# Normalised tokens prepared by chunks of features instead of by tiles of tokens, and one vector made piece by piece, in a two-part transformer block

## The chip, the cores and the metric

The kernel runs on one core of a Trainium2 chip. The metric is the device time of one execution in microseconds. A core has a matrix engine (TensorE, PE in the profile; its weight loads are listed apart as PEld), VectorE (DVE), ScalarE (ACT), GpSimd (POOL) and SyncE (SP), which here only issues DMA transfers. Each engine works through its own row of instructions in order and waits on semaphores for the others. PE writes to PSUM, eight banks of 128 x 512 float32; the other data lie in SBUF, 128 partitions wide.

## The reference, cut to what matters

2048 tokens of 512 features (float32), one batch. `c` gives six vectors of 512 that shift, scale and gate.

```python
mod = (silu(c) @ w_mod).reshape(1, 6, 1, -1)
sa, ca, ga, sb, cb, gb = (mod[:, i] for i in range(6))
h = layernorm(x) * (1 + ca) + sa
x = x + ga * A(h, wq, wk, wv, wo, beta)
h = layernorm(x) * (1 + cb) + sb
x = x + gb * (relu(h @ w1 + b1) ** 2 @ w2 + b2)
# A: 32 heads of 16; the tokens in 4 segments of 512. In a segment: softmax attention with a mask,
# mixed by a gate with a read of a memory (M, z) that the earlier segments' keys and values have filled
# through phi(t) = t + 1 if t > 0 else exp(t); then the segment adds its own. At the end @ wo
```

The change is in the third line: how `layernorm(x) * (1 + ca) + sa` gets into the form that the products with `wq`, `wk` and `wv` read, and how `sa` is made.

## The kernel before, in words

**Numbers in two halves.** A product of float32 matrices is made from operands split in a high part (rounded by a copy to the type float32r) and a low part (what is left). Three matmuls add up: high x high, high x low, low x high.

**Segments and units.** The 512 tokens of a segment lie in four tiles of 128. A segment has four units of eight heads, so there are 16 units `u = 4*s + cc`. For each unit `qk` projects queries and keys (banks `bqk`), `vproj` makes the values of a segment (`bv`), `a_quad` computes scores for the row maxima (`ba`), `b_quad` the scores again, transposed, their exponentials (`pt`) and the products with the values (`bpv`), and `mem` reads and updates the memory (`bmr`, `bpkt`, `bmu`). Two other streams run beside this: `make_w1` prepares combinations of blocks of `w1` in the buffer `X1L`, each cast to a high part by ACT (line 747) and stored to `w1d` in DRAM, and the projected output of a segment goes to DRAM. After the last segment come `wo`, the second normalisation and the feed-forward part (`bh`, `bpf`), from about 440 us to the end.

**The first normalisation** (`ln1`). For each tile of 128 tokens DVE takes the statistics (`ln_stats`), POOL the reciprocal root, and DVE normalises in place (`ln_apply`; tile `xt`). Then `ln_transposed`, tile by tile: PE turns the four 128 x 128 blocks of the tile into one bank `blnq`; the result has the features on the partitions, in KD = 4 chunks of 128. Scale and shift then differ by partition and chunk, so `ln_affine` needs one instruction for each chunk, 128 columns wide: in segment 0 two on ACT and two on DVE, in the other segments all four on ACT (`lnf`). `ln_split` copies the high part into `HT` (ACT) and subtracts for the low part (DVE in segment 0, POOL later). `HT` is `[P, 2, KD, L]`: high and low, four chunks, 512 tokens. There is one `HT`, so the copies of a segment wait for all projections of the segment before (`HUSE[s - 1]`), and the projections wait for all eight halves (`HTN[s]`). Only unit 0 is different: it is made in two halves of 256 tokens.

**Scale and shift** (`mod_cols`). `mod_parts` multiplies the columns of `c` with `w_mod` in four column groups at once (bank `bmod`, 4 matmuls of 512 columns), ACT copies the four partial rows out, and four matmuls against a selecting column add them up and turn them (bank `bmodc`, 1 column each). This is done for the multiplier (`ca`, 1) and for the added vector (`sa`, 0).

**Order.** `Plan` holds every piece of work as a node with its engine, its predecessors and the buffers that it takes and gives back. The order in which an engine's nodes are written out comes from `ORDER`, a table of node numbers for each of PE, ACT, DVE, POOL and SP. At run time each engine keeps to that order, whatever is ready. `N_WARM = 70` nodes on PE are warm-ups, matmuls of the unit matrix that nobody reads (`bwarm`, line 542); the table places them, too. A product on half of the array's rows (projections and scores) waits, where the second turn begins, for a one-element copy on ACT (`fence`).

Of the kernel before, what the change touches and what calls it, by code (L numbers as in the profile page):

```python
# [17 lines left out]
P = 128  # L18
D = 512
# [38 lines left out]
8-32 3 33-43 94 86 117 96 88 111 44-47 123 48-49 105 50-77 280 290 281-282 291 283-286 292 287 293-297 447-449 333-334  # L58
450 335-336 868 452-454 350 364 455 873 338-340 371 341 379 606-609 385 361 392 611-612 358 613 355 614 316-319 376
367 321 551 322 476 481 323-324 382 732 397 733 400 388 734 404 735 490 407 737 497 738 505 412 878 883 508 739 484  # L60
740 487 416-418 395 420 427 554 522 502 423 430 524 493 435 439 677 635 511 440-441 640 887 556 888 646 563 889 559
890 443 566 892-893 643 571 894 514 895 649 656 530 575 680 576-577 670 579 532 586 1056 589 664 1057 582 1058 652
1059 761 769 803 1061-1062 594 775 598 806 546 599-600 682 996 689 1063-1064 692 920 667 921-922 661 923 548 766 685
925 673 926 772 697 927 782 928 790 778 701-703 705 602 937 712 938 954 939 962 715 940 1131 708 942 968 943 720
944-945 793 1481 724 1191-1192 808 796 1193-1194 787 999 1196-1197 811 799 1198-1199 975 989 725 1002 726 815 959 818
965 823 827 1266 980 831 828-829 834 1326 838 846 1327 971 1328 1089 1329 986 841 1486 1471 1331 983 1332-1333 1134
1097 1334 992 1476 728 1110 850 1137 851 1005 1124 852 1100 1118 1269 1008 1012 854 1015 1094 1024 1103 1020 1028 1025
1115 1035 1272 1026 1031 1106 1121 1038 1224 1235 1043 1047 1232 1238 1140 1048-1049 1143 1490 1147 1127 1491 1155
1150 1492 1229 1493 1051 1245 1159 1253 1163 1160-1161 1404 1166 1495 1170 1496 1259 1173 1497 1241 1498 1178 1401
1359 1182-1184 1275 1256 1540-1541 1282 1250 1542-1543 1278 1186 1285 1545-1546 1290 1364 1547 1262 1548 1380 1373  # L70
1523-1524 1367 1525 1388 1407 1294-1296 1370 1298 1526 1305 1385 1528 1301 1529 1391 1313 1530 1376 1531 1394 1659
1557 1660-1661 1565 1662 1308 1599 1664 1571 1665 1397 1666-1667 1602 1562 1317-1319 1794 1410 1413 1795 1321 1796
1578 1797 1586 2079 1568 1799 1417 1800 1425 1801 1574 1420 1802 1589 1592 2084 1429 1605 1430-1431 1734 1692 2074
1697 1929 1433 1930 1440 1931 1583 1436 1932 1443 1448 1703 2089 1452 1608 1595 1934-1935 1611 1700 1936 1713 1937
1706 1737 1453 1718 1615 1740 1454 1724 1618 1869 1623 1627 1721 1631 1709 1628-1629 1634 1727 1638 1641 1456 1872
1646 1650 1827 1835 1743 1651 1875 1652 1841 1750 2093 1753 1730 2094 1832 1746 2095 1758 2096 1848 1838 1762 1654
1766 1763-1764 1862 1769 2098 1856 1773 2099 1776 2100 1844 2101 1859 1781 2004 1785-1787 2007 1962 2122 1853 1878
2123 1885 2124 1865 1970 2125 1983 1888 2127 1789 1976 2128 1893 2129-2130 2251 1967 2252 1881 2253-2254 1973 2198
1997 538 1897-1899 1991 1901 2256 1908 2257 1979 2258 2156 1994 2259 2139 1904 2140 1988 2141 2161 2142 1911 2167 2144
2000 2145 1916 2170 2146-2147 2177 2191 1920-1922 540 2013 2188 2375 2016 2376 2164 2020 2377 2023 2378 1924 2185 2028  # L80
2380-2381 2173 2382 2301 2306 2383 2322 2182 2032-2034 2036 2499 2043 2500 2046 2309 2501 2194 2502 2315 2280 2504
2039 2505 2312 2506 2051 2285 2055 2201 2507 2288 2204 2056-2057 2291 2208 2318 2211 2059 2216 2220 2224 2227 2221
2231 2294 2010 2222 2234 2446 2239 2641 2243 2404 2297 2244-2245 2418 2651 2644-2647 2409 2325 2328 2654-2655 2661
2415 2332 2335 2656-2657 2340 2412 2247 2425 2344-2346 2348 2355 2439 2664 2671 2665-2667 2351 2421 2674 2681
2675-2677 2363 2528 2542 2684-2685 2721 2686 2536 2430 2358 2724 2687 2725-2727 2691 2436 2533 2449 2367-2369 2433
2456 2464 2694-2695 2731 2696-2697 2442 2459 2452 2371 2734 2701 2735 2774 2736 2549 2563 2539 2737 2468-2470 2472
2545 2479 2704-2705 2560 2475 2482 2706-2707 2487 2573 2554 2766 2741 2770 2762 2491-2493 2557 2576 2580 2744-2746
2583 2566 2570 2495 2588 2747 2711 2592 2596 2603 2593 2599 2606 2611 2714-2717 2751 2594 2615-2617 2754 2619
# [131 lines left out]
2396 2524 2680 2523 2525 2517 2670 2700 2720 2520 2519 2740 2522 2730 2424 2526 2690 2445 2710 2838 2548 2569 2750  # L220
2796-2797 2839 2843 2828 2798 2818 2884 2808 2847 2856 2848 2852 2861 2865 2857 2866 2874 2901 2875 2879 2870 2883
2893 2888 2892 2897 3167-3173 3424-3426 3379 3427-3430 3681-3682 3388 3131 3683 3639 3125 3645 3122 3684 3636 3685
3642 3382 3385 3128 3686-3687 3893 3896 3902 3899
""",
}

# [1394 lines left out]
```

## Time and profile before

| | |
|---|---|
| median of 3 runs | 764.79 us (761.73 to 765.94) |
| profiled execution | 762.98 us |
| its span, first to last instruction | 761.3 us |
| mean granted clock of PE | 0.995 |
| busy: PE, DVE, ACT, POOL | 749.7, 582.7, 440.1, 322.3 us |

The granted clock is the share of full speed that the chip allows PE. A row of the profile's lists names the line of the kernel, the engine, the operation and `out<-in` by the names of the tiles, with a count, times in us unless marked ns, and, behind a bar or in brackets, the idle time of that engine just before and what ended it. The chain that ended last is followed back from the last instruction, at each step to what released it. Windows give busy time by stretches of the span. A float32 matmul is recorded as two passes, so that 70 warm-ups are 140 records. Times of PE's records overlap a little; distances from start to start are safer to add up.

### The profile page before, as it was taken

How to read it: one execution, taken by the hardware profiler on the slowest of the kernel's cores; microseconds unless marked ns; L12 is line 12 of the kernel's file. 1: busy time of each engine (PE TensorE's matmuls, PEld its weight loads, DVE VectorE, ACT ScalarE, POOL GpSimd, SP SyncE). 2: the span in 40 equal slices, each digit the busy share in tenths (PEclk: the TensorE clock that was granted, in tenths of full speed). 3: DMA queues.
4: the chain of work that ended last, by engine and by line, in shares of the span. 5: the costliest groups of instructions: out<-in, count | busy, mean ns of one | idle time of the engine just before them, and what ended most of it. 6: DMA issues, size and time to landing. Idle time of an engine off the chain costs nothing.

```text
span 761.3 us, 18032 instructions
## 1 busy us (share of the span) xinstructions
PE 749.7 (98%) x6649; PEld 598.1 (79%) x6649; DVE 582.7 (77%) x1591; ACT 440.1 (58%) x1001; POOL 322.3 (42%) x400
## 2 busy tenths in 40 slices
PE   9999999999999999999999999999999999999997
PEld 8977676666687667766676679998998899989986
DVE  4587789888899788989989887868855875577544
ACT  2669888899878998678856844636111321221110
POOL 4667777677778777474422542350002002000000
PEclk9999999998999999999999999999999999999999
DMA  9587873554654425355753156753555254448621
GB/s 309 171 239 213 247 206 99 154 148 134 167 161 128 113 80 153 105 141 167 235 170 126 44 194 241 269 200 135 194 194 193 103 208 189 158 161 275 242 92 55
DMA packets 61057, 129.65 MB, mean 170 GB/s; under 512 B 8613, under 2 KB 23977, under 8 KB 59178
## 3 DMA queue, kind: packets, MB, share of 16 engines
q1 hardware_dynamic: 60818, 128.37, 52.8%
q8 instruction: 53, 0.87, 0.5%
q14 instruction: 34, 0.28, 0.1%
q10 hardware_dynamic: 152, 0.13, 0.1%
HBM read 81.29 MB, written 20.19 MB: 133 GB/s over the span
## 4 chain that ended last, share of the span: by engine, by line
PE 86%; ACT 4%; DMA 3%; SPq 2%; POOL 2%; issue 2%; DVE 1%; ACTq 0%; POOLq 0%; DVEq 0%
PE bh L1501 18%; PE bpv L1131 8%; PE bqk L796 7%; PE bpf L1564 7%; PE bpf L1563 7%; PE bpf L1565 7%; PE bpb L1072 5%; PE ba L903 5%; PE bv L869 5%; PE bwop L1233 2%; PE bwarm L542 2%; DMA w1d<-X1L 2%; PE bwop L1235 2%; PE bwop L1234 2%; PE blnq L613 2%
## 5 line engine op out<-in xcount | busy, mean ns | idle before, releaser
L908 DVE CUSTOM_DVE_ANT_0 ba<-ba,msk 128x384 f32<-128x384 f32 (+2 forms) x384 | 192.8, 531 | 34.5 <-PE ba L903 21.3
L1089 ACT ACTIVATE pt<-bpb 128x512 f32<-128x512 f32 x320 | 172.4, 621 | 18.4 <-PE bpb L1072 15.8
L1076 POOL TENSOR_SCALAR_AFFINE_SELECT pt<-pt 128x512 f32<-128x512 f32 x128 | 80.3, 645 | 84.2 <-ACT pt L1089 69.7
L796 PE MATMUL bqk<-HT,WQK 64*128 64x512 f32 x720 | 103.4, 398 | 0.0
L1131 PE MATMUL bpv<-pt,VT 128*32 128x512 f32 (+3 forms) x1024 | 81.5, 441 | 1.4 <-ACT pt L1089 0.9
L1072 PE MATMUL bpb<-ST 64*128 64x256 f32 (+2 forms) x512 | 78.5, 351 | 1.7 <-DVE mx L908 1.2
L796 PEld LDWEIGHTS bqk<-HT,WQK 64*128 64x128 f32 x720 | 68.8, 185 | 10.7 <-DVE mx L908 1.2
L903 PE MATMUL ba<-ST 63*128 63x256 f32 (+2 forms) x512 | 75.1, 346 | 1.5 <-ACT pt L1089 0.7
L1332 POOL TENSOR_TENSOR tt<-h2raw 128x512 f32<-128x512 f32 x8 | 10.9, 1367 | 142.6 <-ACT h2raw L1297 98.6
L1072 PEld LDWEIGHTS bpb<-ST 64*128 64x128 f32 x512 | 51.9, 189 | 21.4 <-ACT pt L1089 4.8
L903 PEld LDWEIGHTS ba<-ST 63*128 63x128 f32 x512 | 48.1, 187 | 24.0 <-ACT pt L1089 5.4
L1527 ACT COPY p<-bh 128x256 f32<-128x256 f32 x28 | 10.4, 371 | 93.1 <-PE bh L1501 64.9
L1501 PEld LDWEIGHTS bh<-ST,w 128*128 128x128 f32 x420 | 56.5, 189 | 3.5
L1501 PE MATMUL bh<-ST,w 128*128 128x256 f32 x420 | 59.0, 282 | 0.0
L1501 PE MATMUL bh<-ST 128*128 128x256 f32 x420 | 58.4, 282 | 0.0
L1501 PEld LDWEIGHTS bh<-ST 128*128 128x128 f32 x420 | 55.8, 190 | 3.1
L908 DVE DVE_READ_ACCUMULATOR2_ANT mx<- 128x1 f32 x384 | 54.2, 141 | 0.0
L1131 PEld LDWEIGHTS bpv<-pt,VT 128*32 128x32 f32 x1024 | 28.2, 109 | 32.8 <-issue 23.0
L1563 PE MATMUL bpf<-w,ST 128*128 128x512 f32 x136 | 53.8, 395 | 0.0
L1545 ACT CAST ST<-xx 128x512 fp32r<-128x512 f32 x43 | 26.1, 619 | 47.6 <-DVE xx L1537 19.1
L1564 PE MATMUL bpf<-w,ST 128*128 128x512 f32 x136 | 53.6, 394 | 0.0
L869 PE MATMUL bv<-WVO,HT 64*128 64x512 f32 x384 | 53.2, 396 | 0.0
(211 smaller groups left out, 1671.1 us busy)
## 6 DMA issues: line engine op xcount, KB each, us to landing
ST<-w1d SPq DMA_DIRECT2D x14, 1792.0 KB
w<-w1d SPq DMA_DIRECT2D x14, 1792.0 KB
ST<-sg SPq DMA_DIRECT2D x192, 128.0 KB
w1d<-X1L SPq DMA_DIRECT2D x21, 512.0 KB
xt<-in_A_x SPq DMA_DIRECT2D x16, 256.0 KB
wm<-in_w_mod SPq DMA_DIRECT2D x16, 256.0 KB
xw<-in_A_x SPq DMA_DIRECT2D x16, 256.0 KB
X1L<-in_B_w SPq DMA_DIRECT2D x7, 512.0 KB
```

The costliest lines, as they stand in the source:

```text
L796: nc.tensor.matmul(bank(banks[w]), W3(w, k, x, cols.start, cols.stop)[r], HT[r, y, k], start=turn == k == i == 0, stop=turn == 1 and k == ...
L869: nc.tensor.matmul(bank(banks[t]), HT[r, x, k, (t2 + t) * P:(t2 + t + 1) * P], WVO[r, k, y], start=turn == k == i == 0, stop=turn == 1 and ...
L903: nc.tensor.matmul(dst[:, c0:c0 + n], ST[b:b + 63, 0, sl, qt * P:(qt + 1) * P], ST[b:b + 63, 1, sl, :n], start=True, stop=True)
L908: nc.vector.tensor_tensor_reduce(i, i, msk[:, 512 - n:], scale=1.0, scalar=-3e38, op0=ALU.add, op1=ALU.max, accum_out=o)
L1072: nc.tensor.matmul(dst, ST[b:b + 64, 1, sl, kb * P:(kb + 1) * P], ST[b:b + 64, 0, sl, q0:512], start=True, stop=True)
L1076: nc.gpsimd.affine_select(out=ap, in_=ap, pattern=[[0, ap.shape[1]], [1, P]], compare_op=ALU.is_ge, fill=0.0, base=0, channel_multiplier=-1)
L1089: ns = [op("ACT", 0.49, lambda j=j: nc.scalar.activation(buf("PPP"[n], pt)[:, i + j], bank(keys[j]), AF.Exp, scale=0.25), pr[slot] + 0.01 ...
L1131: nc.tensor.matmul(bank(o)[32 * hq:32 * hq + 32, q0:q0 + src.shape[1]], v[:, a:a + 32], src, start=start, stop=stop, tile_position=(0, 32 ...
L1501: nc.tensor.matmul(pb(i), A[:, x, kk], B[:, y, kk], start=kk == j == 0, stop=kk == 1 and j == 2)
L1563: nc.tensor.matmul(q, rh, wh, start=(i == 0), stop=False)
L1564: nc.tensor.matmul(q, rh, wl, start=False, stop=False)
L1565: nc.tensor.matmul(q, rl, wh, start=False, stop=(i == NF - 1))
```

## The change

**By chunks.** `ln1` normalises all four tiles first. Then `ln_chunk`, for each chunk of 128 features: PE turns this chunk's block of all four tiles into one bank (still 16 transposes in a segment), one instruction scales and shifts all 512 tokens (ACT; in segment 0 DVE for chunks 1 and 3), ACT copies the high part and DVE or, from segment 1, POOL subtracts. A turn now waits for the normalisation of all four tiles.

**Readers.** A projection's products with chunk `k` wait for that chunk alone (`HTK[s][k]`), and a chunk's high half waits only for the last readers of the same chunk in the segment before (`HKUSE[s - 1][k]`). `chunk` sets in which order a segment reads the chunks, up or down, so that the chunk that is read last differs from segment to segment. Unit 0 reads 512 tokens at once: 24 matmuls of 512 columns in place of 48 of 256.

**Added vector.** `mod_pieces` makes `sa` without the detour: as each 128 rows of `w_mod` have landed, four matmuls with one column of `c` add to four columns of a bank, 16 in all, weights 128 x 128; there is no copy by ACT.

**Order.** All five tables are new, 3894 nodes in place of 3905. Three places show how.

At the start, PE, from the first product for `bmod` on, before. `blnq` is the bank of the turned blocks, `bqk` of the projections:

```order
L570 MATMUL bmod<-wmod,cs 32x512 x8
L613 MATMUL blnq<-ident,xt 128x128 x4
L592 MATMUL bmodc<-selc,t 128x1 x8
L613 MATMUL blnq<-ident,xt 128x128 x4
L542 MATMUL bwarm<-ident 128x128 x4
L613 MATMUL blnq<-ident,xt 128x128 x4
L542 MATMUL bwarm<-ident 128x128 x2
L613 MATMUL blnq<-ident,xt 128x128 x4
L542 MATMUL bwarm<-ident 128x128 x28
L788 MATMUL bqk<-HT,WQK 128x256
```

The same place now, from the last of the pieces on:

```order
L608 MATMUL bmodc<-cs,wmod 128x1 x4
L542 MATMUL bwarm<-ident 128x128 x3
L570 MATMUL bmod<-wmod,cs 32x512 x4
L542 MATMUL bwarm<-ident 128x128 x4
L592 MATMUL bmodc<-selc,t 128x1 x4
L640 MATMUL blnq<-ident,xt 128x128 x16
L542 MATMUL bwarm<-ident 128x128 x23
L804 MATMUL bqk<-HT,WQK 128x512 x3
L542 MATMUL bwarm<-ident 128x128 x11
L804 MATMUL bqk<-HT,WQK 128x512 x3
L542 MATMUL bwarm<-ident 128x128 x3
L804 MATMUL bqk<-HT,WQK 128x512 x3
```

The sixteen turns now stand together, behind the multiplier's two steps. Of the 70 warm-ups 28 stand ahead of `bmod` (36 before), 27 between it and the first projections (34 before), and 15 among the products of the first chunks (none before).

ACT in the normalisation of segment 2, before. `X1L` is the cast for the feed-forward weights, `pk`, `mt`, `ac`, `sg` are copies for the memory, the maxima, the scores and the projections:

```order
L747 CAST X1L<-X1L 128x256
L1089 ACTIVATE pt<-bpb 128x512 x2
L619 ACTIVATE lnf<-blnq,modc 128x128 x8
L1024 COPY pk<-bpkt 128x4x64 x2
L747 CAST X1L<-X1L 128x512
L970 ACTIVATE mt<-bat 16x64 x2
L626 CAST HT<-lnf 128x4x128
L619 ACTIVATE lnf<-blnq,modc 128x128 x4
```

The same place now:

```order
L644 ACTIVATE lnf<-blnq,modc 128x512
L763 CAST X1L<-X1L 128x256
L1039 COPY pk<-bpkt 128x4x64
L650 CAST HT<-lnf 128x512
L1039 COPY pk<-bpkt 128x4x64
L985 ACTIVATE mt<-bat 16x64 x2
L650 CAST HT<-lnf 128x512
L951 COPY ac<-ba_2750 128x512
L951 COPY ac<-ba_2749 128x512
L650 CAST HT<-lnf 128x512
L841 CAST sg<-bqk 128x512 x2
L763 CAST X1L<-X1L 128x512
```

The 512-column cast of `X1L` has moved behind three copies to `HT`, two to `ac` and two to `sg`.

PE in the normalisation of segment 1, before, the third and fourth tile's turns:

```order
L1072 MATMUL bpb<-ST 128x256 x4
L613 MATMUL blnq<-ident,xt 128x128 x8
L903 MATMUL ba_1058<-ST 128x512
L903 MATMUL ba_1059<-ST 128x512
L796 MATMUL bqk<-HT,WQK 128x512 x6
```

Now three of the four chunks' turns stand in one piece, ahead of other score products:

```order
L1087 MATMUL bpb<-ST 128x256 x2
L1087 MATMUL bpb<-ST 128x384 x2
L640 MATMUL blnq<-ident,xt 128x128 x12
L918 MATMUL ba_965<-ST 128x256
L918 MATMUL ba_966<-ST 128x256
```

The first two tiles' turns stood far earlier before, apart from each other; now no turn stands before the fourth tile is normalised.

The diff, without the tables:

```diff
@@ ORDER @@
-8-32 3 33-43 94 86 117 96 88 111 44-47 123 48-49 105 50-77 280 290 281-282 291 283-286 292 287 293-297 447-449 333-334
+8-24 3 25-28 94 29 95-96 30-32 97 33-35 86 36-39 88 117 121 109 113 40-62 283 63-73 284 74-76 285 77 277-280 286
...
+    def mod_pieces(m, slot, plus, pr):
+        key, b = ("wmod", m), ("modc", m)
+        loads, n = [], None
+        for k in range(KD):
+            loads.append(sp(lambda k=k: nc.sync.dma_start(buf("P", key)[:, k] if not k else TL[key][:, k],
+                                                          wmod[k * P:(k + 1) * P, m * D:(m + 1) * D]),
+                            pr + 0.001 * k, 1 << 18, get=() if k else [("P", key)], soft=loads[:1]))
+
+        def mm(k):
+            for j in range(KD):
+                nc.tensor.matmul(bank(b)[:, j:j + 1], TL[key][:, k, j * P:(j + 1) * P], cs[:, k:k + 1],
+                                 start=k == j == 0, stop=k == j == KD - 1)
+        for k in range(KD):
+            n = pe("F", 1.05, lambda k=k: mm(k), pr + 0.02 + 0.001 * k, after=[n_cs, loads[k], n], get=() if k else [("#D", b)],
+                   put=[key])
+        return dve(4, lambda: nc.vector.tensor_scalar(modc[:, slot, :], bank(b)[:, 0:KD], plus, None, op0=ALU.add),
+                   pr + 0.05, after=[n], put=[b])
...
+    def ln_chunk(s, k, pr, applied, wait):
+
+        b, f = ("lnq", s, k), ("lnf", s, k)
+        keys = [("xt", 4 * s + t) for t in range(4)]
+
+        def turn():
+            for t in range(4):
+                nc.tensor.transpose(bank(b)[:, t * P:(t + 1) * P], TL[keys[t]][:, k * P:(k + 1) * P], ident)
+        n = pe("F", 0.357, turn, pr, after=applied, get=[("#D" if s else "#A", b), ("oraw", f)], put=keys)
+        sc, bi = modc[:, CA, k:k + 1], modc[:, SA, k:k + 1]
+        if s or k % 2 == 0:
+            n = act(512, lambda: nc.scalar.activation(buf("oraw", f), bank(b), AF.Identity, scale=sc, bias=bi), pr + 0.01,
+                    after=[n, *MODC[CA]], put=[b])
...
+            n = dve(512, lambda: nc.vector.tensor_scalar(buf("oraw", f), bank(b), sc, bi, op0=ALU.mult, op1=ALU.add), pr + 0.01,
+                    after=[n, *MODC[CA]], put=[b])
+        eng, e = (nc.gpsimd, "POOL") if s else (nc.vector, "DVE")
+        h = act(512, lambda: nc.scalar.copy(HT[:, 0, k], TL[f]), pr + 0.02, sbuf=True, after=[n, *wait], put=[f])
+        l = op(e, 1.24 if s else 0.6, lambda: eng.tensor_tensor(HT[:, 1, k], TL[f], HT[:, 0, k].bitcast(F32), op=ALU.subtract), pr + 0.03,
+               after=[h], put=[f], lock=True)
         return [h, l]
...
-    n_sa = mod_cols(0, SA, 0.0, PR0 + 0.2, True)
+    n_sa = mod_pieces(0, SA, 0.0, PR0 + 0.2)
...
+    HTK, HKUSE = {}, {s: [[] for _ in range(KD)] for s in range(-1, NS)}
+
+    def chunk(s, turn, i):
+
+        return KD - 1 - i if (s + turn) % 2 else i
...
+        HTK[s] = {}
+        for i in range(KD):
+            k = chunk(s, 0, i)
+            HTK[s][k] = ln_chunk(s, k, p_turn[i], ap, HKUSE[s - 1][k])
...
-                    n = pe("R", 0.697, lambda turn=turn, k=k: half(turn, KD - 1 - k if turn else k), pr[turn] + 0.002 * k,
-                           after=[n] if n else [*HTN[s], *(z for w in (0, 1) for z in (WN[w, cc] if s == 0 else []))],
...
+                    n = pe("R", 0.697, lambda turn=turn, k=k, i=i: half(turn, k, turn == i == 0, turn == 1 and i == KD - 1), pr[turn] + 0.002 * i,
+                           after=[n, *(HTK[s][k] if not turn else ()),
...
-            for i in range(0 if u else 2):
-                c = slice(i * L // 2, (i + 1) * L // 2)
...
+            for k in range(0 if u else KD):
+                n = done[w] = pe("F", 0.697, lambda w=w, k=k: mm(w, k), pr[w] + 0.002 * k,
+                                 after=[done.get(w), *HTK[0][k], *(WN[w, cc] if k == 0 else []), *([] if k or w else [n_w0])],
```

`vproj` is changed in the same way as `qk`.

393 lines of the change are left out of this document (182 added, 211 removed), and 14 rows, old and new, of the table ORDER.

## The prediction

> **What bounds the kernel now.** I read the page first: span, busy time and the shares of the chain that ended last.
>
> ```profile
> span 761.3 us, 18032 instructions
> ...
> PE 749.7 (98%) x6649; PEld 598.1 (79%) x6649; DVE 582.7 (77%) x1591; ACT 440.1 (58%) x1001; POOL 322.3 (42%) x400
> ...
> PE 86%; ACT 4%; DMA 3%; SPq 2%; POOL 2%; issue 2%; DVE 1%; ACTq 0%; POOLq 0%; DVEq 0%
> ```
>
> PE is the bound almost everywhere: 98% busy, 86% of the chain. So the change can gain only where PE runs slowly or the chain leaves it, and it loses wherever it adds to PE. Next I cut the span into windows. The columns are window, length, busy time (and instructions) of PE, PEld, DVE, ACT and POOL, granted clock, DMA share, GB/s.
>
> ```profile
> 60.00:80.00 20.00, 19.64 (x241) 13.66 (x237) 17.26 (x59) 19.89 (x53) 14.33 (x16) 1.00 0.80 239
> ...
> 160.00:180.00 20.00, 18.84 (x232) 10.55 (x229) 16.32 (x63) 17.55 (x40) 13.73 (x20) 0.83 0.37 107
> ...
> 240.00:260.00 20.00, 20.00 (x218) 13.98 (x216) 15.62 (x48) 19.53 (x48) 15.44 (x18) 1.00 0.49 129
> 260.00:280.00 20.00, 19.62 (x284) 12.37 (x284) 17.06 (x65) 20.00 (x48) 16.26 (x23) 1.00 0.19 45
> 480.00:520.00 40.00, 40.00 (x261) 36.34 (x260) 29.06 (x59) 22.83 (x45) 17.40 (x15) 1.00 0.64 230
> ```
>
> ACT is full at 60 to 80 and at 240 to 280 us, and at 160 to 180 the granted clock is only 0.83. These are the three places where segments 1, 2 and 3 are normalised. In the feed-forward part (480 to 520) PE has no idle time and nothing to win. The chain in order of time (start, length, what) runs through the scaling of the normalised tokens, tile `lnf`, at all three:
>
> ```profile
> 69.03 1.90 ACT lnf L619 x6
> ...
> 70.93 0.89 ACT lnf L619 x2
> ...
> 163.03 0.82 ACT lnf L619 x3
> ...
> 163.97 0.44 ACT lnf L619
> ...
> 258.52 1.50 ACT lnf L619 x4
> ```
>
> That is 5.55 us of the chain in 16 instructions, four groups of four. The slow clock comes in two steps; finer windows show them:
>
> ```profile
> 160.20:163.60 3.40, 2.92 (x40) 1.74 (x36) 3.19 (x14) 2.56 (x9) 3.04 (x5) 1.00 0.84 212
> 163.60:167.00 3.40, 3.01 (x70) 1.44 (x62) 1.58 (x4) 3.07 (x8) 2.98 (x7) 1.00 0.67 217
> 167.00:169.90 2.90, 2.61 (x20) 1.45 (x16) 2.83 (x12) 2.90 (x7) 1.07 (x1) 0.99 0.03 6
> 169.90:173.30 3.40, 3.40 (x31) 2.50 (x30) 2.95 (x13) 3.38 (x9) 1.64 (x3) 0.50 0.00 0
> 173.30:176.70 3.40, 3.40 (x19) 1.42 (x18) 2.64 (x9) 2.26 (x6) 2.47 (x3) 0.50 0.00 0
> ```
>
> PE is idle for 0.48, 0.39 and 0.29 us in three windows running, and then for 6.8 us the clock is at half. PE's timeline names who was late, and ACT's what held it:
>
> ```profile
> 162.47 0.60 PE L903 MATMUL ba<-ST 63*128 63x256 f32 x4 [0.47 <-ACT mt L970]
> ...
> 164.46 0.46 PE L1033 MATMUL bmu<-VT,pk 128*32 128x34 f32 x32 [0.39 <-ACT lnf L619]
> ...
> 167.81 1.12 PE L903 MATMUL ba<-ST 63*128 63x512 f32 x5 [0.27 <-ACT pt L1089]
> ```
> ```profile
> 156.12 0.41 ACT L747 CAST X1L<-X1L 128x256 fp32r<-128x256 f32 x1
> ...
> 157.40 2.90 ACT L619 ACTIVATE lnf<-blnq,modc 128x128 f32<-128x128 f32 x8
> ...
> 161.68 0.62 ACT L747 CAST X1L<-X1L 128x512 fp32r<-128x512 f32 x1 [0.84 <-DMA w1d<-X1L]
> ```
>
> All three waits are for ACT, behind eight scalings in a row and a cast that waits 0.84 us for a store of feed-forward weights to land.
>
> **The change, part by part.** *Added vector by pieces.* Before, both vectors took two steps on PE:
>
> ```profile
> 12.43 1.92 PE L570 MATMUL bmod<-wmod,cs 128*32 128x512 f32 x16
> ...
> 14.78 1.84 PE L592 MATMUL bmodc<-selc,t 128*128 128x1 f32 x16
> ...
> 18.73 0.60 PE L613 MATMUL blnq<-ident,xt 128*128 128x128 f32 x4
> ...
> 19.17 6.42 PE L542 MATMUL bwarm<-ident 128*128 128x128 f32 x56
> ...
> 22.66 1.93 DVE L626 TENSOR_TENSOR HT<-lnf,HT 128x512 fp32r<-128x512 f32 x3 [0.30 <-ACT HT L626]
> ...
> 25.34 0.36 PE L788 MATMUL bqk<-HT,WQK 128*128 128x256 f32 x1
> ```
>
> Each row holds two vectors, so one vector cost 0.96 + 0.92 = 1.9 us. The pieces are 16 matmuls of the second row's own form (it shows 8, at two passes each): 16 x 1.84/8 = 3.7. PE does 1.8 us more. Does the start hide that? The warm-ups are fixed in number and order: 70 before, 70 after. So PE's stream up to the first projections is a sum, and what is added to it comes out behind it, unless PE waits less. It waited a little: the first row's 1.92 for 16 passes holds about 0.5 of waiting for late loads, while the pieces' loads now come first. I take +1.3 (bounds: +0.5, if all overlaps well; +1.8, if nothing is saved).
>
> *First projection over whole chunks.* 48 matmuls of 256 columns become 24 of 512. They ran from 25.34 to just after this row's last start:
>
> ```profile
> L790 PE MATMUL bqk<-HT,WQK x16: 279/283/283, 25.7 to 31.0; 128*128 128x256 f32 x16
> ```
>
> 5.7 us for 12,288 columns; the same columns again, so 0 (bounds -0.2, 0). Is `HT` ready in time? Before, 24.6 - 18.7 = 5.9 us passed from the last turn to the last low half (rows above). After, 23 warm-ups, at 6.42/28 = 0.23 each 5.3 us, lie before the first chunk's products, and 15 more among them; with three chunks' products (0.7 each) 10.8 us lie before the last chunk's. So readiness is covered, and the 15 warm-ups are time that PE spends although the operands are there. If that cover were gone, PE would wait, and warm-ups would only trade places with idle time.
>
> *Fourth tile's load.* It moves from sixth to tenth in SP's queue, behind four more loads of 0.26 MB.
>
> ```profile
> 8.81 0.66 DVE L600 BATCH_NORM_STATS2 bs<-xt 128x6 f32<-128x512 f32 x1
> ...
> 10.00:20.00 10.00, 10.00 (x90) 8.51 (x90) 3.94 (x11) 4.24 (x11) 1.22 (x4) 1.00 1.09 357
> ```
>
> At 357 GB/s that is 2.9 us later: statistics at 11.7. Before, 8.81 to the end of the last normalisation at 12.7 took 3.9 us, so now 15.6. PE reaches the turning, which now needs all four tiles, only after the multiplier's two steps, which ended 14.78 + 0.92 = 15.7 and now end later by the pieces. 0, with little to spare: what a late tile costs beyond that pushes the warm-ups behind the turning and all that follows.
>
> *Scaling, segments 1 to 3.* Four instructions of 128 columns become one of 512. The four take
>
> ```profile
> 241.24 1.50 ACT L619 ACTIVATE lnf<-blnq,modc 128x128 f32<-128x128 f32 x4
> 242.62 2.07 ACT L1089 ACTIVATE pt<-bpb 128x512 f32<-128x512 f32 x4
> ...
> L619 ACT ACTIVATE lnf<-blnq,modc x56: 434/462/580, 16.9 to 259.6; 128x128 f32<-128x128 f32 x56
> ```
>
> 1.38 us from start to next start, 0.345 each though one lasts 0.462. The casts above cost 0.62 - 0.41 = 0.21 us per 256 columns more, so 512 columns last 0.46 + 0.31 = 0.77, less the same overlap of 0.12: 0.65 (bounds: 0.48, as L1089's four step, and 1.38, no gain). One group saves 0.73, three segments 8.8 us of ACT. Only the four groups on the chain count at first: -2.9 (bounds: 0, if what stands beside them is late by as much; -5.5, if all of it leaves the chain).
>
> *The half clock.* By the order, the cast that waited 0.84 us now stands behind three copies to `HT` and two score copies, and ACT has only two scalings there. I expect PE's three waits to shrink and the 6.8 us at half clock to go. In its first half ACT was busy 3.38 of 3.40 us, so PE would find no faster supply; in the second, 2.26, so half of 3.4 us is to be had: -1.7 (bounds: 0 and -3.4).
>
> *Release by chunks, order anew.* The high halves wait only for their own chunk's last readers, but the copies stand in ACT's row where ACT is full, so 0 (bound: -1.5, the three copies' share near 72 us). In the feed-forward part the rows are permuted and PE has no idle time to lose or win: 0. Counted over the whole order, PE changes between whole-array, row-half and column-quarter work 153 times, 160 before. One such change is bounded by the same two transposes ahead of a column product and ahead of a row product:
>
> ```profile
> 270.90 0.25 PE bat L968 x2
> ...
> 281.69 0.06 PE bat L968 x2
> ```
>
> At most 0.19, so seven fewer give 0 to -1.3; I take -0.7.
>
> **Sum.** The profiled execution took 762.98 us (span 761.3, 1.7 around it): 762.98 + 1.3 - 2.9 - 1.7 - 0.7 = 759.0. The median of the runs shown is 764.79, 1.8 above that execution, the fastest 1.3 below; I let 759.0 stand for the median too, well inside the range. A measurement of this kernel tells from no change what exceeds about 0.5%, 3.8 us: below 761.0 is faster, above 768.6 slower.
>
> **The rivals.** *Clock stays.* The half clock is not owed to these waits, and remains: 759.0 + 1.7 = 760.7. For it: no idle stretch of PE there is longer than 0.48 us. Against: the three idle windows stand right ahead of it, and the other windows above, with less idle time in them, have the full clock. [...]
>
> *Absorbed.* ACT gets faster, and the chain moves to its neighbours: DVE is busy 17.26 and 17.06 us of the windows at 60 and 260. Then only PE's own terms remain: 762.98 + 1.3 - 0.7 = 763.6, no change.
>
> *Slower: the turn as a barrier.* A chunk's turn needs all four tiles, so a late normalisation on DVE holds PE, in whose row attention stands behind the 8 or 12 transposes. From the point where such a wait leaves PE idle for half a microsecond in windows running, as at 160, it brings its 0.5 and half clock at full price, 3.4. Two of the three segments: 763.6 + 2 x 3.9 = 771.4. For it: DVE is nearly full there, and the blocks of turns are now larger. Against: before, this is all that PE's turns waited for a normalisation (us, times), out of 32 turns:
>
> ```profile
>   DVE xt L609: 0.4, 1
> ```
>
>
> *More.* All bounds of gain in ACT and clock: 762.98 + 1.3 - 5.5 - 3.4 - 1.3 = 754.1.
>
> **How the numbers follow.** Forecast 0.40, clock stays 0.12, absorbed 0.23, barrier 0.20, more 0.05. Faster: 0.35 + 0.07 + 0.05 = 0.47, since the first two lie close to the limit; same: 0.05 + 0.05 + 0.20 = 0.30; slower: 0.20 + 0.03 = 0.23. The range takes in the absorbed case and the bounds of gain, and ends where a single barrier stands (763.6 + 3.9 = 767.5, with a spread of 1.5): 753 to 769 leaves out most of the last-but-one case. The forecast's own range, by its terms' bounds, is 754 to 763.
>
> **What would show it.** Right: first projections end near 32.4 us; scalings at about 0.65 each; ACT below 19 of 20 us near 70 and 260; no window at half clock between 60 and 280 us. Wrong: PE waits ahead of `blnq`; half clock at 0.50 at any place; chain shares of DVE or DMA that grow by what ACT's lose.

## The result, and the profile after

The changed kernel takes 765.88 us (median of 20 runs, 763.63 to 772.11), the kernel before, beside it on the same chips, 762.50 us (median of 20, 761.43 to 765.94). The ratio is 1.0045 with a 95% interval of 1.0030 to 1.0059: slower by 3.4 us, where 759.0 and "faster" had been forecast. By the bound set in the prediction (0.5%) it is just within "no change"; by the interval it is a loss. All ratios and intervals below come from fast runs alone (one run of the pieces alone, 773.74 us, counts as slow) and are not the quotients of the medians shown. The profiled execution took 769.3 us, among the longer ones.

The page of the changed kernel, span, busy times and the chain's shares by engine:

```profile
span 767.6 us, 17957 instructions
...
PE 753.6 (98%) x6641; PEld 607.3 (79%) x6641; DVE 585.1 (76%) x1585; ACT 431.4 (56%) x958; POOL 321.5 (42%) x400
...
PE 86%; ACT 4%; DMA 3%; SPq 2%; POOL 2%; DVE 1%; issue 1%; ACTq 0%; POOLq 0%; DVEq 0%
```

ACT has 8.7 us less to do, as the scaling promised, and the chain's shares are what they were. PE is busy 3.9 us longer, though it has 8 records fewer. The windows (the same columns as in the prediction) say why; the third number from the end is the granted clock:

```profile
10.00:20.00 10.00, 10.00 (x61) 8.11 (x60) 2.40 (x6) 1.10 (x2) 2.20 (x3) 0.66 1.09 359
20.00:30.00 10.00, 10.00 (x73) 9.87 (x73) 5.70 (x8) 7.17 (x13) 1.75 (x2) 0.82 0.49 170
...
60.00:80.00 20.00, 17.79 (x186) 13.90 (x182) 15.84 (x52) 16.46 (x41) 7.86 (x10) 1.00 0.79 222
160.00:180.00 20.00, 19.85 (x242) 12.66 (x238) 17.81 (x64) 19.14 (x44) 16.46 (x20) 1.00 0.44 128
260.00:280.00 20.00, 19.52 (x258) 12.21 (x254) 16.34 (x59) 19.74 (x47) 14.28 (x19) 1.00 0.48 129
```
```profile
296.60:300.00 3.40, 2.53 (x20) 1.44 (x13) 2.65 (x7) 3.24 (x8) 0.00 (x0) 1.00 0.02 5
300.00:303.40 3.40, 3.40 (x20) 3.35 (x19) 2.96 (x12) 1.93 (x5) 2.00 (x2) 0.50 0.19 39
```

The half clock at 170 us is gone (0.83 before, 1.00 now), as forecast. But there is a new one in the start, 0.66 and 0.82 where the kernel before has 1.00 in both windows (the prediction shows the first, the second is below), and a short one at 300 us behind a window in which PE idled 0.87 of 3.40 us. From the kernel before:

```profile
20.00:30.00 10.00, 10.00 (x89) 10.00 (x89) 4.89 (x9) 6.70 (x14) 7.53 (x6) 1.00 0.61 219
```

In the trace's record of the clock the half clock in the start lasts from 13.28 to 23.52 us: 10.24 us at 0.50, in which PE does the work of 5.1. PE's timeline there (start, length, what, how many passes) shows what ran:

```profile
9.20 0.95 PE L608 MATMUL bmodc<-cs,wmod 128*128 128x1 f32 x8
10.01 0.47 PE L542 MATMUL bwarm<-ident 128*128 128x128 f32 x2
10.31 1.84 PE L608 MATMUL bmodc<-cs,wmod 128*128 128x1 f32 x16
12.02 0.91 PE L542 MATMUL bwarm<-ident 128*128 128x128 f32 x6
12.77 1.24 PE L608 MATMUL bmodc<-cs,wmod 128*128 128x1 f32 x8
...
19.16 1.71 PE L592 MATMUL bmodc<-selc,t 128*128 128x1 f32 x8
20.73 3.30 PE L640 MATMUL blnq<-ident,xt 128*128 128x128 f32 x16
23.86 5.30 PE L542 MATMUL bwarm<-ident 128*128 128x128 f32 x46
28.92 0.94 PE L804 MATMUL bqk<-HT,WQK 128*128 128x512 f32 x3
29.69 2.62 PE L542 MATMUL bwarm<-ident 128*128 128x128 f32 x22
...
34.37 3.69 PE L804 MATMUL bqk<-HT,WQK 128*128 128x512 f32 x15
```

PE never idles between 9 and 38 us (29.00 us busy of 29.00). The one-column pieces (L608) run from 9.2 to 14.0, the clock halves at 13.28, and eight passes of one column, 0.95 us at full clock, take 1.24 across the step and 1.71 behind it (L592, the multiplier's second step). Unit 0's first projections end at 38.1 us; 32.4 was forecast.

**Clock and the rest, apart.** A run's mean granted clock tells how much time the half clock took: (1 - clock) x 765 us. For the profiled execution (0.991) that gives 6.9 us; its trace has 13.65 us at half clock, a loss of 6.8. So each comparison below can be split. The split is rough: the mean takes in the end of a span, too, where the trace of the kernel before has 0.50 from 760.4 us on, where PE has nothing left to do: 0.85 us, counted as 0.4 us of loss. Over its runs the changed kernel has a mean clock of 0.9954 (3.5 us lost). For the 20 runs of the kernel before that stood beside it no clock is on record; its 32 runs beside the next experiments have 0.9976 (1.8 us lost). By these, of the 3.4 us 1.7 is clock and 1.7 is something else.

### The profile page after: what moved, and what is told of

It reads as the page before. It is cut to its first block, busy times and chain, and to the rows that moved or that the text cites. A ratio compares the mean times of both kernels' runs of the same rounds, so it can differ in the third digit from the quotient of the medians.

```text
span 767.6 us, 17957 instructions
## 1 busy us (share of the span) xinstructions
PE 753.6 (98%) x6641; PEld 607.3 (79%) x6641; DVE 585.1 (76%) x1585; ACT 431.4 (56%) x958; POOL 321.5 (42%) x400
## 4 chain that ended last, share of the span: by engine, by line
PE 86%; ACT 4%; DMA 3%; SPq 2%; POOL 2%; DVE 1%; issue 1%; ACTq 0%; POOLq 0%; DVEq 0%
PE bh L1516 18%; PE bqk L810 9%; PE bpv L1146 7%; PE bpf L1579 7%; PE bpf L1578 7%; PE bpf L1580 7%; PE bpb L1087 5%; PE bv L880 5%; PE ba L918 5%; PE bwarm L542 3%; PE bwop L1248 2%; ACT pt L1104 2%; PE bwop L1250 2%; PE bwop L1249 2%; PE bmr L1011 1%
## 5 line engine op out<-in xcount | busy, mean ns | idle before, releaser
L810 PE MATMUL bqk<-HT,WQK 64*128 64x512 f32 x720 | 105.7, 397 | 0.0
L810 PEld LDWEIGHTS bqk<-HT,WQK 64*128 64x128 f32 x720 | 70.6, 185 | 9.1 <-issue 0.9
L918 PEld LDWEIGHTS ba<-ST 63*128 63x128 f32 x512 | 51.0, 186 | 17.9 <-issue 6.5
L880 PE MATMUL bv<-WVO,HT 64*128 64x512 f32 x384 | 56.5, 404 | 0.7 <-DVE mx L923 0.7
L1578 PE MATMUL bpf<-w,ST 128*128 128x512 f32 x132 | 52.1, 395 | 0.0
L1579 PE MATMUL bpf<-w,ST 128*128 128x512 f32 x132 | 52.0, 394 | 0.0
L1580 PE MATMUL bpf<-w,ST 128*128 128x512 f32 x132 | 51.7, 391 | 0.0
```

What stands on the lines that cost most here:

```text
L810: nc.tensor.matmul(bank(banks[w]), W3(w, k, x, cols.start, cols.stop)[r], HT[r, y, k], start=first and i == 0, stop=last and i == 2)
L880: nc.tensor.matmul(bank(banks[t]), HT[r, x, k, (t2 + t) * P:(t2 + t + 1) * P], WVO[r, k, y], start=first and i == 0, stop=last and i == 2)
L918: nc.tensor.matmul(dst[:, c0:c0 + n], ST[b:b + 63, 0, sl, qt * P:(qt + 1) * P], ST[b:b + 63, 1, sl, :n], start=True, stop=True)
L1578: nc.tensor.matmul(q, rh, wh, start=(i == 0), stop=False)
L1579: nc.tensor.matmul(q, rh, wl, start=False, stop=False)
L1580: nc.tensor.matmul(q, rl, wh, start=False, stop=(i == NF - 1))
```

## The experiments

**Theory 1.** The pieces cost. Their one-column products bring the half clock in the start, and they are work that PE's start has to do. **Theory 2.** The new order costs: loads and stores that come late at 64 to 80, 300 to 320 and 361 to 368 us hold PE, and the pieces do not matter.

### Each half of the change alone

The pieces alone, in the order of the kernel before:

```
-    n_sa = mod_cols(0, SA, 0.0, PR0 + 0.2, True)
+    n_sa = mod_pieces(0, SA, 0.0, PR0 + 0.2)
```

> The kernel before with the added vector by pieces alone: one-column products among the warm-ups of the start, everything else and its order as before. Theory 1: 1.3 to 1.8 us more work of TensorE and one to three windows of half clock in the first 30 us, 1.003 to 1.007 of the time before. Theory 2: no half clock that was not there before, 1.000 to 1.002 of the time before.

Measured: ratio 1.0081 (1.0055 to 1.0107), just above Theory 1's range; the medians are 770.87 and 762.36 us, with runs from 762.2 to 773.7. The start has the half clock, 0.73 and 0.93:

```profile
10.00:20.00 10.00, 10.00 (x68) 8.67 (x67) 2.17 (x5) 0.16 (x1) 1.08 (x3) 0.73 1.09 361
20.00:30.00 10.00, 10.00 (x84) 9.17 (x81) 5.52 (x13) 7.63 (x17) 2.96 (x2) 0.93 0.60 215
```

The changed kernel without the pieces, the same line the other way round, chunks and new order kept:

> The changed kernel with the added vector made as before in one go (eight products of eight weights each, early in the start), the turning by chunks and the new order kept. Theory 1: TensorE has some 1.3 us less in its start and no half clock there, so the half clock of 13.3 to 23.5 us is gone, unit 0 ends 3 to 5 us earlier than in the changed kernel, and the time is 0.998 to 1.000 of that before. Theory 2: the late loads stay, and the time is 1.0025 to 1.0045 of that before.

Measured: 759.91 us, ratio 0.9964 (0.9949 to 0.9979), and a granted clock of 0.999 or 1.000 in each of 11 runs; that is below Theory 1's range. The two halves multiply to the whole: 1.0081 x 0.9964 = 1.0045. So the pieces cost 6.2 us in either order, and everything else in the change gains 2.7. Theory 2 had 1.0025 to 1.0045 here and is out as the main cause. In the trace unit 0's first products run at

```profile
22.98 0.95 PE L804 MATMUL bqk<-HT,WQK 128*128 128x512 f32 x3
...
28.44 3.69 PE L804 MATMUL bqk<-HT,WQK 128*128 128x512 f32 x15
```

and start 5.94 us earlier than in the changed kernel (28.92). Of these 5.94 us 5.1 are its half clock, and 0.8 is left for the pieces' work.

By the means over the runs, the pieces' 6.2 us split into 4.7 of clock (0.9914 against 0.9976) and 1.5 for the rest in the order of before, and into 3.2 of clock (0.9954 against 0.9995) and 2.9 for the rest in the new order. What that rest is beyond the 0.8 us of the traces is open.

### One column and the clock

Here one thing in the kernel before was changed: the last 28 warm-ups stream one column in place of 128.

```
-  nc.tensor.matmul(bank(wk_)[:, :P], ident, ident, start=True, stop=True)
+  nc.tensor.matmul(bank(wk_)[:, :n], ident, ident[:, :n], start=True, stop=True)   # n = P if i < 42 else 1
```

> The kernel before with one thing changed: the last 28 warm-up products of the start (19.2 to 25.6 us) multiply one column in place of 128, with the same weights and the same number of instructions; TensorE has no longer pauses than before. Theory 1 (the clock control counts columns that stream, not instructions): one or two windows of half clock, each 3.4 us, begin between 20 and 30 us, and the time rises by 1.7 to 5 us, 1.002 to 1.007 of that before. Rival (the clock falls only where TensorE is idle): no half clock in the start and 0.999 to 1.001 of the time before.

Measured: 765.92 us, ratio 1.0045 (1.0023 to 1.0066). PE's timeline, and windows cut at the steps of the clock:

```profile
19.68 7.85 PE L542 MATMUL bwarm<-ident 128*128 128x1 f32 x56
27.39 0.56 PE L788 MATMUL bqk<-HT,WQK 128*128 128x256 f32 x1
```
```profile
20.00:24.17 4.17, 4.17 (x39) 4.17 (x39) 3.82 (x8) 4.10 (x9) 2.94 (x2) 1.00 1.05 380
24.17:27.58 3.41, 3.41 (x18) 3.41 (x18) 1.61 (x3) 2.72 (x6) 1.65 (x2) 0.50 0.47 166
27.58:31.00 3.42, 3.42 (x17) 3.42 (x18) 0.00 (x0) 0.00 (x0) 3.31 (x3) 0.50 0.03 7
```

PE and its weight loads are busy all the time, and 4.5 us after the one-column products begin the clock is at half for 6.83 us. The mean clock of the runs is 0.9919 against 0.9972: 4.1 us of clock for a loss of 3.4. By the profile's records, then, the clock does not fall only where PE is idle. Apart from the ends of the spans, the stretches of half clock with known steps last 3.41, 6.83 or 10.24 us: 10.24 and 3.41 in the changed kernel, 6.83 in the kernel before (169.90 to 176.73) and in the start here, 3.41 in the start without the 15 warm-ups (below). Why these lengths, no run shows.

The complement is the changed kernel with each piece's product made against 128 equal columns, one of them used:

```
-  nc.tensor.matmul(bank(b)[:, j:j + 1], ..., cs[:, k:k + 1],
+  nc.tensor.matmul(bank(b)[:, j * P:(j + 1) * P], ..., cs[:, k:k + 1].to_broadcast([P, P]),
```

> The changed kernel, but each one-column product of the added vector is made against 128 equal columns, of which one is used: same weights, same number of instructions, about 8 times 128 columns more of streaming in place of 8 times 1. Theory 1 (the one-column products leave TensorE looking idle to the clock control, and the half clock from 13.3 to 23.5 us is their doing): the half clock in the first 30 us is gone or cut to at most one window of 3.4 us, and the start is 2 to 4 us shorter than in the changed kernel, so about 0.999 to 1.002 of the time before. Theory 2 (the loss comes from loads that the new order brings late, at 64 to 80, 300 to 320 and 361 to 368 us, and the pieces do not matter): the half clock may go or stay, and the time stays at 1.0045 of that before, or rises by the extra columns.

Measured: 763.66 us, ratio 1.0013 (0.9993 to 1.0034), in Theory 1's range and between the changed kernel and the one without pieces. The start runs at full clock, and eight passes of 128 columns cost hardly more than eight of one (1.06 here, 0.95 above):

```profile
10.00:20.00 10.00, 10.00 (x90) 9.04 (x90) 3.77 (x9) 2.29 (x4) 2.19 (x3) 1.00 1.09 360
20.00:30.00 10.00, 10.00 (x83) 9.59 (x81) 4.62 (x6) 7.85 (x16) 5.89 (x5) 1.00 0.55 169
```

So with 128 times the columns the start is shorter: unit 0's first product starts at 24.47 us, against 28.92. Against the changed kernel the gain is 0.3%, 2.4 us with an uncertainty of some 2. Against the kernel without pieces (0.9964) 0.5% remains, 3.7 us with an uncertainty of some 2; clock has 0.4 us of it (mean 0.9990 and 0.9995). In the two traces unit 0's first product starts 1.49 us later, of which 0.37 already stands ahead of the pieces (8.45 against 8.08); the other 1.1 us are the pieces' own extra work. The remainder is open.

The same in the order of the kernel before:

> The kernel before with the added vector by pieces, each piece multiplied against 128 equal columns of which one is used. By the runs so far the pieces alone, with one column each, cost 0.81% of the kernel before. Theory 1 (half clock from the one-column products, plus some 1.3 us more work of TensorE in the start): no half clock in the first 30 us, and 1.001 to 1.003 of the time before, so most of the 6 us goes. Theory 2 (the pieces cost by where they stand and what waits behind them, whatever the clock): 1.006 to 1.009 as with one column.

Measured: 767.58 us, ratio 1.0062 (1.0043 to 1.0081). The start has no half clock (1.00 in the first 30 us), but the expected gain did not come: the time is the one that Theory 2 gave, and from the one-column form (1.0081) the intervals overlap. Mean clock is 0.9952, since half clock shows up at 174.7 us in the trace (0.87 in the window from 160 to 180, 0.96 from 180 to 200), where the kernel before has it too. The rest, 3.1 us, is more than the 1.5 found above and like the 2.9 in the new order. In its trace the first product of unit 0 starts at 28.29 us instead of 25.34. Of these 2.95 us 0.66 lies in the first 50 warm-up passes (8.46 us, 7.80 before), which differ from trace to trace (7.75 to 8.66 in the five in this order); in that of the kernel before they go at 0.22 us a pass up to 6.06 us and at 0.11 after. How much of the 3.1 is the pieces' work and how much such luck, these runs do not settle.

### The warm-ups

The prediction called the 15 warm-ups among unit 0's products time that PE spends although the operands are there. Without them (55 in place of 70), in the kernel without pieces:

> The kernel of the run before it (added vector in one go, chunks and new order kept), without the 15 warm-up products that the changed kernel has in the middle of unit 0's projections: 55 warm-ups in place of 70. Theory 1, by which the warm-ups are a fixed sum on TensorE's own path: 15 times 0.11 to 0.23 us goes, so 1.7 to 3.4 us less than with all 70, and 0.994 to 0.998 of the time before; unless the clock falls to half for want of them, which costs 1.7 us for each window of 3.4 us. Theory 2: the start does not set the end, and the time is that of the run with all 70 warm-ups.

Measured: 758.95 us, ratio 0.9946 (0.9927 to 0.9965); the gain over 0.9964 is 0.2%, less than the uncertainty. In the traces unit 0's 24 first products take 9.08 us with the 15 warm-ups and 7.25 without, of which 1.30 is a wait; so the warm-ups take 3.1 us. Two rows without them show why that isn't won:

```profile
27.32 3.24 PE L804 MATMUL bqk<-HT,WQK 128*128 128x512 f32 x13 [1.30 <-POOL WQK L724]
...
33.55 0.73 PE L880 MATMUL bv<-WVO,HT 64*128 64x512 f32 x4 [0.48 <-POOL WVO L724]
```

The split weights, made behind the halves of the tokens, come 1.30 and 0.48 us after PE is ready. The warm-ups had covered that; by the traces 1.3 us of them was pure loss.

With the pieces kept, the 15 warm-ups were taken away in one run and placed between the pieces in another. PE's row of the second, before (as in the changed kernel) and now (warm-ups by number, pieces by name):

```
changed kernel: 17 warm, cs, 4 warm, piece, 1 warm, 2 pieces, 3 warm, piece, 3 warm, ...
spread:         17 warm, cs, 4 warm, piece, 4 warm, piece, 4 warm, piece, 6 warm, piece, 8 warm, ...
```

> The changed kernel without those 15 warm-ups, 55 in place of 70; its pieces stay as they are. Theory 1: the half clock of the start stays, or grows by a window since the cover behind it is shorter; against that up to 1.4 us less waiting-time filled by warm-ups (what the same step gave without the pieces), so 1.001 to 1.005 of the time before, and not faster than the run with all 70 warm-ups spread between the pieces, though TensorE has 3.4 us less to do. If only TensorE's work in the start counts: 1.5 to 3.4 us less than the changed kernel, 1.000 to 1.0025, and faster than the spread.

> The changed kernel with its 70 warm-ups and its one-column pieces, but the 15 warm-ups that stood among unit 0's projections now stand between the pieces, so that one-column products fill at most about half of any 3.4 us. Theory 1 (the half clock comes from windows filled with one-column products): no half clock in the start or one window less of it, 1.7 to 5 us less than the changed kernel where that one has it, and 0.998 to 1.002 of the time before. If the share of one-column products does not matter: half clock as in the changed kernel, or the 15 warm-ups cost 3.4 us on the other side of unit 0's first product, and 1.004 to 1.007.

Measured: 761.42 us without the 15, ratio 0.9978 (0.9960 to 0.9996); 765.36 us with them spread, 1.0041 (1.0014 to 1.0068). The first is below both ranges, the second in the range of the other reading; Theory 1 had the order of these two the wrong way round. The half clock behaves as it said: with the 15 gone 3.41 us of it stay in the start (13.61 to 17.02 us in the trace, 0.83 in the window from 10 to 20), with them spread there is none:

```profile
10.00:20.00 10.00, 10.00 (x89) 9.04 (x89) 2.50 (x6) 0.81 (x2) 0.94 (x2) 1.00 1.08 358
20.00:30.00 10.00, 10.00 (x82) 9.58 (x81) 5.98 (x8) 8.34 (x17) 4.01 (x3) 1.00 0.54 173
...
31.72 3.28 PE L804 MATMUL bqk<-HT,WQK 128*128 128x512 f32 x13 [1.31 <-POOL WQK L724]
```

But the spread warm-ups stand ahead of unit 0's products and cover nothing: PE waits 1.31 us for the split weights again, although the whole start is 4.4 us later than without pieces and without the 15 warm-ups. That wait moves along with the tokens' halves. So it isn't enough to keep the clock up; work of PE in the start still costs time. How the 15 warm-ups, 1.3 us net in the traces, come to 0.67% (5.1 us, with an uncertainty of 1.8) with the pieces and 0.2% (1.4, uncertainty 1.9) without, is open.

In the kernel before, 8 of the last 28 warm-ups were taken away:

> The kernel before without the last 8 of its 70 warm-ups, which run from 23.5 to 25.3 us, right ahead of the first projections. Theory 1 (the start is a sum of TensorE's own work): the first projection starts 1.8 us earlier, and the time is 0.997 to 0.998 of that before. Rival (the halves of the turned tokens or the split weights set the start): the warm-ups' place is taken by a wait of the same length, and the time is 0.9995 to 1.0005 of that before.

Measured: 761.44 us, ratio 0.9985 (0.9969 to 1.0000), between the two ranges. Of the 1.8 us the projections that follow unit 0's first ones got 0.5 in the trace; the tokens' halves are late:

```profile
24.04 0.38 PE L788 MATMUL bqk<-HT,WQK 128*128 128x256 f32 x1 [0.28 <-ACT HT L626]
24.93 0.39 PE L789 MATMUL bqk<-HT,WQK 128*128 128x256 f32 x1 [0.51 <-DVE HT L626]
...
160.00:180.00 20.00, 18.86 (x240) 10.31 (x240) 17.84 (x64) 19.54 (x46) 14.60 (x21) 1.00 0.37 110
```

The last row, a window of the same trace, is worth a look. PE is busy 18.86 of 20 us, to 0.02 what it was in the profiled execution of before (18.84), and yet the clock stays at 1.00. The three waits are there (0.26, 0.39 and 0.30 us for the same three products, 0.47, 0.39 and 0.27 before). The same waits stand ahead of half clock in one execution and not in another.

### Scaling and order

The forecast's largest gain is the scaling of 512 tokens at once. In the kernel without pieces each one on ACT was made as four of 128 again:

```
-  nc.scalar.activation(buf("oraw", f), bank(b), AF.Identity, scale=sc, bias=bi)
+  o = buf("oraw", f)
+  for t in range(4):
+      c = slice(t * P, (t + 1) * P)
+      nc.scalar.activation(o[:, c], bank(b)[:, c], AF.Identity, scale=sc, bias=bi)
```

> The changed kernel with the added vector in one go (0.9964 of the time before so far), and each scaling of 512 columns made as four of 128, as before the change. It tells the price of the scaling by itself, which the prediction put at 2.9 us. If that holds: 2 to 3 us more than with whole scalings, 0.999 to 1.001 of the time before, perhaps with the half clock near 170 us back. If ScalarE's time is hidden: 0.996 to 0.997.

Measured: 768.05 us, ratio 1.0056 (1.0038 to 1.0075), 0.92% or 7.0 us above the whole scalings, where 2 to 3 were expected. PE's waits in that run name `lnf` (total, times, longest); these four rows add up to 4.7 us, and with whole scalings the only such row has 0.2:

```profile
PE ba L923 <- ACT lnf L648: 1.6, 3, 0.9
...
PE bmu L1053 <- ACT lnf L648: 1.3, 1, 1.3
PE bpv L1151 <- ACT lnf L648: 1.0, 1, 1.0
PE bpb L1092 <- ACT lnf L648: 0.8, 2, 0.5
```

So whole scalings are worth more than 2.9 us in the new order, yet with them chunks and order together gain only 2.7. The new order, with four scalings, costs 4.3 us against the kernel before: it has been drawn up for whole ones. Where it loses in one execution shows in wide windows of the kernel before and of the one without pieces:

```profile
40.00:160.00 120.00, 118.02 (x1350) 86.14 (x1349) 101.69 (x329) 101.91 (x256) 85.26 (x96) 1.00 0.66 192
160.00:240.00 80.00, 77.14 (x908) 55.08 (x904) 69.51 (x235) 67.10 (x162) 61.74 (x84) 0.96 0.53 148
240.00:320.00 80.00, 79.58 (x952) 56.94 (x950) 67.33 (x229) 70.93 (x170) 55.92 (x74) 1.00 0.42 117
```
```profile
40.00:160.00 120.00, 116.88 (x1336) 88.07 (x1336) 102.06 (x332) 98.11 (x235) 81.98 (x96) 1.00 0.63 181
160.00:240.00 80.00, 79.61 (x961) 57.52 (x957) 72.12 (x243) 70.71 (x168) 66.17 (x86) 1.00 0.56 159
240.00:320.00 80.00, 77.58 (x941) 57.61 (x939) 68.71 (x229) 66.85 (x155) 52.12 (x67) 1.00 0.41 112
```

PE idles 1.1 us more up to 160, 2.5 less from 160 to 240, and 2.0 more from 240 to 320. The gain lies where segment 2 is normalised. Among the losses are waits for late transfers; up to 160 us the two longest waits are 1.36 us for the copy of the maxima and 1.30 for `pt`, which is ACT's. Two late transfers are the copies of the transposed maxima at 73 us (a wait of 1.47 us in the run without the 15 warm-ups) and of the split queries near 310 (1.47 us with all 70 warm-ups, 0.48 us of idle time in the window at 300 without the 15). Two moves in SP's row put them ahead, from the kernel with 55 warm-ups:

```
SP near 67 us:  - X1L load, ST copy, w1d store, ST<-mt x2
                + ST<-mt x2, X1L load, ST copy, w1d store
SP near 303 us: - w1d store, 3 ST copies, o_dram store, 3 ST copies
                + 6 ST copies, o_dram store, w1d store
```

> The changed kernel with the added vector in one go and 55 warm-ups (0.9946 of the time before so far), and two moves in the new order of SyncE's queue: the two copies of the transposed maxima that TensorE waited 1.47 us for at 73 us are issued ahead of a weight load, a copy and a store, and one store of weights and one of outputs at 302 to 306 us go behind the copies that TensorE waited for there (0.48 us in its trace). If the new order's late transfers are on the path that sets the end: 1 to 2 us less than without the moves, 0.992 to 0.993 of the time before. If what they delay is made up later: 0.994 to 0.995.

Measured: 757.82 us, ratio 0.9938 (0.9920 to 0.9956), against 0.9946 without the moves: 0.6 us, inside the uncertainty, so which of the two readings holds is not decided. Ahead of the same products, first without and then with the moves:

```profile
73.09 0.67 PE L1087 MATMUL bpb<-ST 64*128 64x512 f32 x2 [1.47 <-DMA ST<-mt]
```
```profile
73.57 0.59 PE L1087 MATMUL bpb<-ST 64*128 64x512 f32 x2 [0.94 <-ACT mt L985]
```

The transfer no longer ends last; the maxima themselves, on ACT, do, with 0.5 us less of waiting, and in the window at 300 PE is busy 20.00 of 20. It is the fastest version here, 4.7 us below the kernel before and 8 below the changed one.

### The runs in one table

Time against the kernel before (ratio - 1, of 762.5 us), the part of it that is clock (mean clock of the runs against that of the kernel before beside them, x 765; for the changed kernel see above), and the rest. The uncertainty of a time is 1.1 to 2.1 us:

| kernel | us | clock | rest |
|---|---|---|---|
| changed | +3.4 | +1.7 | +1.7 |
| before + pieces | +6.2 | +4.7 | +1.5 |
| before + pieces of 128 columns | +4.7 | +1.6 | +3.1 |
| before, 28 warm-ups of one column | +3.4 | +4.1 | -0.7 |
| before, 62 warm-ups | -1.1 | -1.0 | -0.1 |
| changed, pieces of 128 columns | +1.0 | -1.1 | +2.1 |
| changed, 15 warm-ups spread | +3.1 | -1.4 | +4.5 |
| changed, 55 warm-ups | -1.7 | +0.8 | -2.5 |
| changed without pieces | -2.7 | -1.5 | -1.2 |
| the same, scaling by four | +4.3 | -0.7 | +5.0 |
| the same with whole scalings, 55 warm-ups | -4.1 | -0.9 | -3.2 |
| the same, two moves in SP's row | -4.7 | -1.1 | -3.6 |

## Why the prediction was wrong

*Added vector by pieces, +1.3: mis-sized, and the step that failed.* The step priced the pieces as work of PE at full clock. They cost 6.2 us, in the order of before and in the new one. What the step left out is what such products do to the clock: 4.7 us of the 6.2 in the kernel before, 3.2 in the changed one. In the work itself, eight passes take 0.95 us at full clock, four times that is 3.8, where 3.7 was forecast. But the 0.5 us taken off for waiting was misread: 16 passes of the first row took 1.92 us, and eight of them take 0.99 from start to start in the run with wide pieces, where nothing shows a wait, so the work term should have been 1.8. The cost that isn't clock is 1.5 us in the kernel before and 2.9 in the changed one; the traces of the start show 0.8 of the latter, and the other 2 us are open. The whole term is +6.2, and it alone takes the forecast's gain away: 759.0 with 6.2 in place of 1.3 is 763.9, against 765.9 measured. The sentence that misled is "PE's stream up to the first projections is a sum": so it is, but at a clock that changed with the stream (0.66 and 0.82 in the start with one column, 1.00 in both windows with 128). The row of one-column products in the trace of before (1.84 us) ran at full clock and gave no sign of it.

*The half clock, -1.7: right in its size, its reason not shown.* In the changed kernel without pieces none of 11 runs has a clock below 0.999, and the clock's part is -1.5. Four of the five traces in the order of before have half clock between 160 and 180 us (0.83, 0.96, 0.87 and 0.91 in that window, 1.00 with 62 warm-ups); none of the six in the new order with a window there has (1.00 in each). But that the three waits bring it is not shown: with 62 warm-ups the same waits left the clock whole.

*Scaling, -2.9: the mechanism right, the size too small in the new order, the gain spent elsewhere.* One scaling of 512 lasts 778 ns in the changed kernel (0.77 forecast). In a row of three it takes 0.67 us from start to start (2.12 us in all, 0.65 forecast). Scalings on the chain fall from 5.55 us to 2.26 (1.45 at 152.14 us and 0.81 at 248.82). Undoing it costs 7.0 us, beyond the bound of 5.5.

```profile
L644 ACT ACTIVATE lnf<-blnq,modc x14: 768/778/801, 21.9 to 248.8; 128x512 f32<-128x512 f32 x14
```

*Order anew, 0, and the 15 warm-ups as cover: wrong by some 2 us, with uncertainties of 1 to 2.* Clock apart, chunks and order gain 1.2 us, where scaling and mode changes should have given 3.6; without the 15 warm-ups it is 3.2. The prediction kept the warm-ups as a fixed sum and took the operands for ready behind them; the split weights were not, for 1.8 of the 15 warm-ups' 3.1 us, and the other 1.3 are lost by the trace. For the rest the traces show late transfers at 60 to 80 and 300 to 320 us, of which only part was tried, so that share is argued and not shown.

*Fourth tile's load, first projection over whole chunks, fewer mode changes.* Nothing in the traces speaks against 0, 0 and -0.7, but none was tried alone, so all three stay unproven.

*The rivals.* "Clock stays" fell for 170 us. The turn as a barrier did not come: no wait of PE ahead of `blnq` appears among its longest waits. "Absorbed" came nearest with its number, 763.6, but for another reason. A rival in which the pieces halve the clock was missing, though the prediction looked for half clock in one place and added one-column products in another.

*What would show it.* Of the marks for right, the scaling's step (0.67 us, 0.65 forecast) and the full clock between 60 and 280 us came; ACT is below 19 us of 20 near 70 (16.46) but not near 260 (19.74), and the first projections end at 38.1 us, not 32.4. Of the marks for wrong, half clock at 0.50 came, in the start and at 300 us.

## What to carry to other kernels

One-column products did not hold the clock: in four traces here a stretch of a few microseconds of mostly such products was followed by 3.4 to 10.2 us at half clock, in one of them with PE and its weight loads busy throughout. Streaming 128 equal columns cost hardly more (1.06 against 0.95 us for eight passes) and kept the clock in the start (1.00 from 10 to 30 us); the time gained 2.4 us in the new order, and nothing clear of the uncertainty in the old one. Best here was not to have the pieces at all. Warm-ups are worth what they cover: look for the wait that would stand in their place before counting them as a gain (1.3 us of 3.1 were left here by the traces).

## What the runs showed of the hardware that was not expected

- A product of one column with a weight load of 128 x 128 takes 0.12 us a pass at full clock (0.95 for eight), much as a warm-up of 128 columns does (0.11, 6.42 for 56), but did not hold the clock: 4.5 us into 56 such passes 6.83 us at half clock began, without any idle time of PE.
- The half clock lasted 3.41, 6.83 or 10.24 us, and much the same idle time stood ahead of it in one execution and not in another: 18.86 us busy of 20 with the clock at 1.00 (62 warm-ups), 18.84 with 0.83 (70). The kernel before by itself has runs with a mean clock from 0.992 to 1.000.
- The wait for the split weights moves with the tokens: 1.30 us when unit 0's products start at 23.23 us, 1.31 us when they start at 27.62.
